# Chunk attention into a squared-ReLU FFN on one core: V loads moved from SyncE's queue to ACT's, from the second block on

## The chip, the cores and the metric

The kernel runs on one core of a Trainium2 chip. The metric is the device time of one execution in microseconds (us), as the median of several executions; the kernel before and the kernel under test run in turn on the same chip. The medians are over all runs of a kernel, a few of which were slow (2 of 4 in e7, 3 of 20 in e9b and in e15); the ratios are over fast runs alone. Engines are TensorE (PE; PEld is its weight load), VectorE (DVE), ScalarE (ACT), GpSimd (POOL) and SyncE (SP); "SPq" and "ACTq" in a profile are DMA issues of those two.

## The reference

Attention within chunks of 64 tokens, 8 heads of 64, over 8 x 576 tokens, then a two-layer FFN on the 4608 x 512 result. Cut to what matters:

```python
scores = scale * np.matmul(q_c, k_c.transpose(0, 1, 2, 4, 3))   # chunks of 64 x 64
attn = softmax(scores)                                          # (written out in the original)
out = np.matmul(attn, v_c)
x = out.transpose(0, 2, 1, 3).reshape(4608, 512)
h = np.maximum(x @ w_in, 0.0)                                   # 512 -> 2048
return (h * h @ w_out)                                          # 2048 -> 512
```

All inputs and the output are float32; the kernel computes in bf16.

## The kernel before

Tokens go in groups of 256 and blocks of two groups, 0 to 8. While PE works on the FFN of block j, the attention of block j+1 (`nxt`) is woven into it, and q, k and V of block j+2 (`far`) are loaded, cast and transposed. Each phase is a generator, and one step of it is a slot: `ffn_in` gives 16 slots, `ffn_out` another 16 (slots 16 to 31).

```python
NV = 5                                  # V buffers: 5 groups of even heads
NO = 2 * NV + 1                         # and 11 half-shifted tiles of odd heads
in_pool = tc.tile_pool(name="qk", bufs=5)
ps_ffn = tc.tile_pool(name="ps_ffn", bufs=4, space=PSUM)    # four banks
...
def v_pieces(g):                        # 4 or 5 DMAs a group, rows of 64 floats
    for t, p, m, b, s in runs(g):
        yield lambda ...: nc.sync.dma_start(out=v_even[g % NV][...], in_=v[...])
    for n in ...:
        ...
            yield lambda ...: nc.sync.dma_start(out=v_odd[n % NO][...], in_=v[...])
...
def transpose_qk_dma(g):                # "TD" in the plan: qkb (bf16) -> qkT
    ...
    nc.sync.dma_start_transpose(out=qkT..., in_=qkb...)
...
def transpose_x(g):                     # "XT": two of these a group, from group 6 on
    ...
            nc.sync.dma_start_transpose(out=xTs[j]..., in_=x...)
...
def ffn_in(j, c, n):                    # per slot: 4 matmuls, relu on ACT, square on DVE
    ...
def ffn_out(j):                         # per 4 slots: 16 matmuls into one bank, then
    ...
                o_sb = ffn_pool.tile([128, d_model], FP32, name="o_sb", bufs=4)
                nc.scalar.copy(out=o_sb, in_=o_ps)
                nc.scalar.dma_start(out=out[t0:t0 + 128, :], in_=o_sb)
```

The loop over blocks, for block 2 on:

```python
loads, go_slots = pieces(far), range(32)            # q, k of both groups, then V of both
d = {2: 5, 3: 2}.get(j, 0)
...                     # of nxt, from slot 4 + d: scores (SC), attention times V (AV), XT
for i, g in enumerate(far):
    at(14 + 2 * i, C, g)                            # cast of q and k on GpSimd
    at(19 + 3 * i, TD, g)                           # transpose of q and k by DMA
phases = [ffn_in(j, 0, len(grps) * GT), ffn_out(j)]
```

Every semaphore is set by the compiler. One thing about them: it gives all DMAs that SyncE and ACT issue one of eight completion semaphores, in turn, for both queues together. A DMA may reuse its semaphore only when the DMA eight places earlier has landed, so it waits for that one at its issuer. I call that one its eight-back partner. The traces bear this out: the DMA issues of the two engines carry eight semaphores in turn.

The softmax here doesn't subtract the row's maximum and nothing guards it: scores larger than these inputs give would overflow.

Of the kernel before, what the change touches and what calls it, by code (L numbers as in the profile page):

```python
# [17 lines left out]
def kernel(  # L18
# [9 lines left out]
    nc = tc.nc  # L28
# [46 lines left out]
    def segments(g0, n):  # L75
        while n:
            b, s = divmod(g0, S)
            m = min(n, S - s)
            yield b, s, m
            g0 += m  # L80
            n -= m
# [3 lines left out]
    def runs(g):  # L85

        for t in range(GT // 128):
            p = 0
            for b, s, m in segments(g * GT + t * 128, 128):
                yield t, p, m, b, s  # L90
                p += m

    def qk_pieces(g):
        q_sb = in_pool.tile([128, 2, H, D], FP32, name="q_sb")
        k_sb = in_pool.tile([128, 2, H, D], FP32, name="k_sb")
        qk[g] = (q_sb, k_sb)
        if g < FIRST_DMA_T:

            p = 0
            for b, s, m in segments(g * GT, GT):  # L100
                for dst, src in ((q_sb, q), (k_sb, k)):
                    yield lambda dst=dst, src=src, b=b, s=s, p=p, m=m: nc.sync.dma_start(
                        out=dst.rearrange("p t h d -> p (t h d)")[p:p + m // 2, :].rearrange(
                            "p (h e) -> p h e", h=H),
                        in_=src[b, :, s:s + m, :].rearrange("h (s i) d -> s h (i d)", i=2))
                p += m // 2
            return
        for t, p, m, b, s in runs(g):
            for dst, src in ((q_sb, q), (k_sb, k)):
                yield lambda dst=dst, src=src, b=b, s=s, t=t, p=p, m=m: nc.sync.dma_start(  # L110
                    out=dst[p:p + m, t, :, :],
                    in_=src[b, :, s:s + m, :].rearrange("h s d -> s h d"))

    def v_pieces(g):

        for t, p, m, b, s in runs(g):
            yield lambda t=t, p=p, m=m, b=b, s=s: nc.sync.dma_start(  # L117
                out=v_even[g % NV][p:p + m, t, :, 0:D],
                in_=v[b, 0::2, s:s + m, :].rearrange("h s d -> s h d"))
        for n in {0: [0, 1, 2], 2: [5], 3: [6, 7, 8]}.get(g, [2 * g + 1, 2 * g + 2]):  # L120
            lo, hi = max(0, 128 * n - 64), min(n_tokens, 128 * n + 64)
            p = lo - (128 * n - 64)
            for b, s, m in segments(lo, hi - lo):
                yield lambda n=n, p=p, m=m, b=b, s=s: nc.sync.dma_start(  # L124
                    out=v_odd[n % NO][p:p + m, :, 0:D],
                    in_=v[b, 1::2, s:s + m, :].rearrange("h s d -> s h d"))
                p += m

    def go(pieces):
        for f in pieces:  # L130
            f()
# [180 lines left out]
    def ffn_in(j, c, n):  # L312
        if j not in gTs:
            gTs[j] = ffn_pool.tile([128, n_ft, BT], BF16, name="gT")
        gT, xT = gTs[j], xTs[j]
        for ft in range(n_ft):
            h = ps_ffn.tile([128, 512], FP32, name="ps_ffn")
            for dt in range(n_dt):
                nc.tensor.matmul(  # L319
                    out=h[:, 0:n],  # L320
                    lhsT=w_in_bf[:, dt, ft * 128:(ft + 1) * 128],
                    rhs=xT[:, dt, c:c + n],
                    start=(dt == 0), stop=(dt == n_dt - 1))
            rl = ffn_pool.tile([128, 512], BF16, name="rl", bufs=3)
            nc.scalar.activation(out=rl[:, 0:n], in_=h[:, 0:n], func=AF.Relu)  # L325
            nc.vector.tensor_tensor(  # L326
                out=gT[:, ft, c:c + n], in0=rl[:, 0:n], in1=rl[:, 0:n], op=ALU.mult)
            yield

    def ffn_out(j):  # L330
        gT = gTs.pop(j)
        for tt in range(len(blocks[j]) * GT // 128):
            o_ps = ps_ffn.tile([128, d_model], FP32, name="ps_ffn")
            for ft in range(n_ft):
                nc.tensor.matmul(  # L335
                    out=o_ps,
                    lhsT=gT[:, ft, tt * 128:(tt + 1) * 128],
                    rhs=w_out_bf[:, ft, :],
                    start=(ft == 0), stop=(ft == n_ft - 1))
                if ft == n_ft - 1:  # L340
                    t0 = blocks[j][tt // 2] * GT + tt % 2 * 128
                    if j == len(blocks) - 1 and tt == 2 * len(blocks[j]) - 1:
                        for copy, dma, c in ((nc.scalar.copy, nc.scalar, 0),
                                             (nc.vector.tensor_copy, nc.sync, 256)):
                            o_sb = ffn_pool.tile([128, d_model], FP32, name="o_sb", bufs=4)
                            copy(out=o_sb[:, 0:256], in_=o_ps[:, c:c + 256])
                            dma.dma_start(
                                out=out[t0:t0 + 128, c:c + 256], in_=o_sb[:, 0:256])
                        yield
                        continue  # L350
# [3 lines that stand above are left out]
                if ft % 4 == 3:  # L354
                    yield
# [27 lines left out]
    def pieces(grps):  # L383
        for g in grps:
            yield from qk_pieces(g)
        for g in grps:
            yield from v_pieces(g)
# [27 lines left out]
    for j, grps in enumerate(blocks):  # L415
        nxt = blocks[j + 1] if j + 1 < len(blocks) else []
        far = blocks[j + 2] if j + 2 < len(blocks) else []
        plan = {}

        def at(slot, f, g):  # L420
            plan.setdefault(slot, []).append((f, g))

        if j == 0:
            loads, go_slots = iter(()), []
            for slot, f in ((24, T), (27, SC), (29, AV), (31, XT)):
                at(slot, f, nxt[0])
            at(31, T, nxt[1])
            phases = [ffn_in(0, 0, 512), ffn_out_by_ft(0)]
        elif j == 1:
            go_slots = [*range(17), *range(34, 48)]  # L430
            loads = itertools.chain(pieces(nxt), pieces(far))
            for slot, f in ((2, SC), (6, AV), (11, XT)):
                at(slot, f, grps[1])
            for i, g in enumerate(nxt):
                for slot, f in ((22 + 4 * i, C), (27 + 4 * i, TD), (36, SC), (38 + 2 * i, AV),
                                (42 + 2 * i, XT)):
                    at(slot, f, g)
            phases = [ffn_in(1, 0, 256), ffn_in(1, 256, 256), ffn_out(1)]
        else:
            loads, go_slots = pieces(far), range(32)  # L440
            d = {2: 5, 3: 2}.get(j, 0)
            if j == 2:
                go_slots = [*range(10), *range(18, 32)]
            for i, g in enumerate(nxt):
                for slot, f in ((4, SC), (8, AV), (11, XT)):
                    at(slot + d if f is SC else slot + d + 3 * i, f, g)
            for i, g in enumerate(far):
                at(14 + 2 * i, C, g)
                at(19 + 3 * i, TD, g)
            phases = [ffn_in(j, 0, len(grps) * GT), ffn_out(j)]  # L450
        slot = 0
        for phase in phases:
            for _ in phase:
                if slot in go_slots:
                    for f in loads:
                        f()
                        break
                for f, g in plan.get(slot, []):
                    f(g)
                slot += 1  # L460
        go(loads)
        if j == 1:
            for g in far:
                C(g)
                TD(g)
# [30 lines left out]
```

## Time and profile before

303.29 us was the median of the three runs before the change (300.78 to 303.96). The profiled run took 304.47 us.

| | before |
|---|---|
| span of the profiled run | 302.7 us |
| PE busy | 280.5 us, 93% |
| ACT busy | 130.0 us, 43% |
| PE starts ffn_in of blocks 2 to 8 at (timeline) | 89.58, 120.65, 151.15, 181.30, 212.52, 241.88, 271.24 |
| DMA queue q1 (SyncE), q10 (ACT) | 46.81 MB, 9.83 MB |

A block without a hole takes PE 29.36 us. Idle time of ACT or SyncE costs nothing by itself: what counts is what PE waits for. The lines are in the prediction.

### The profile page before, as it was taken

The numbers are of one execution on the slowest core, as the hardware profiler recorded it, in microseconds if no ns is written. First come the engines' busy times: TensorE is split into PE (matmuls) and PEld (weight loads), VectorE is DVE, ScalarE is ACT, GpSimd is POOL, SyncE is SP. The second block draws the span as 40 slices with busy tenths as digits, with TensorE's granted clock in tenths as the row PEclk, the third lists the DMA queues.
The fourth block names the chain that finished last, engine by engine and source line by source line (L and its number), as shares of the span: only waits on it lengthen the run. The fifth ranks groups of instructions, "written<-read, shape, count | busy, mean of one in ns | idle before, by whom it ended". The sixth has DMA issues, their size and how long they took to land.

```text
span 302.7 us, 6379 instructions
## 1 busy us (share of the span) xinstructions
PE 280.5 (93%) x2564; PEld 141.3 (47%) x2598; DVE 113.0 (37%) x247; ACT 130.0 (43%) x225; POOL 49.4 (16%) x68
## 2 busy tenths in 40 slices
PE   2889979898899799899999997999999999999995
PEld 2654435784454444444444443444444444444442
DVE  1348613692234350353037203740482038104400
ACT  1536305674217621762176215731662186217511
POOL 2047820140130040023003201400230000000000
PEclk9999999999799999999999999999999999999999
DMA  7999999999999899999899899869997704211011
GB/s 207 243 347 365 342 264 246 237 206 212 217 213 211 194 191 205 224 215 193 195 250 211 148 229 269 171 104 254 267 183 157 182 37 37 69 69 38 0 69 69
DMA packets 158765, 57.04 MB, mean 188 GB/s; under 512 B 139664, under 2 KB 152208, under 8 KB 158736
## 3 DMA queue, kind: packets, MB, share of 16 engines
q1 hardware_dynamic: 153024, 46.81, 73.2%
q10 hardware_dynamic: 5712, 9.83, 10.4%
q8 instruction: 20, 0.33, 0.5%
q14 instruction: 9, 0.07, 0.1%
HBM read 36.70 MB, written 9.44 MB: 152 GB/s over the span
## 4 chain that ended last, share of the span: by engine, by line
PE 67%; DMA 18%; SPq 10%; issue 2%; POOL 1%; ACT 1%; DVE 0%; ACTq 0%
PE ps_ffn L319 31%; PE ps_ffn L335 27%; DMA qkT<-qkb 6%; DMA k_sb<-in_k_dram 6%; SPq L224 4%; DMA w_st<-in_moe_w_in_dram 4%; SPq L282 3%; PE ps_att L259 2%; PE ps_ffn L364 2%; DMA w_st<-in_moe_w_out_dram 2%; PE ps_att L238 2%; SPq L117 1%; PE ps_ffn L164 1%; SPq L124 1%; POOL w_in_bf L139 1%
## 5 line engine op out<-in xcount | busy, mean ns | idle before, releaser
L319 PE MATMUL ps_ffn<-xT,w_in_bf 128*128 128x512 bf16 (+1 forms) x620 | 128.6, 357 | 3.1 <-ACT rl L325 1.6
L326 DVE TENSOR_TENSOR gT<-rl 128x512 bf16<-128x512 bf16 (+1 forms) x160 | 75.5, 489 | 133.9 <-ACT rl L325 131.4
L335 PE MATMUL ps_ffn<-w_out_bf,gT 128*128 128x512 bf16 x500 | 113.0, 382 | 0.8 <-issue 0.3
L325 ACT ACTIVATE rl<-ps_ffn 128x512 bf16<-128x512 f32 (+1 forms) x160 | 86.2, 560 | 42.5 <-PE ps_ffn L319 31.0
L319 PEld LDWEIGHTS <-w_in_bf 128*128 128x128 bf16 x640 | 60.8, 98 | 60.9 <-issue 2.1
L335 PEld LDWEIGHTS <-gT 128*128 128x128 bf16 x512 | 49.9, 98 | 59.7 <-issue 1.3
L352 ACT COPY o_sb<-ps_ffn 128x512 f32<-128x512 f32 x31 | 18.2, 586 | 92.9 <-PE ps_ffn L335 79.7
L217 POOL CAST qkb<-q_sb 128x1024 bf16<-128x1024 f32 x14 | 14.7, 1048 | 146.9 <-DMA q_sb<-in_q_dram 126.6
L269 DVE TENSOR_TENSOR x<-ps_att,rec 128x512 bf16<-128x512 f32 x36 | 24.9, 691 | 1.2
L245 ACT ACTIVATE e<-ps_att 128x1024 bf16<-128x1024 f32 x18 | 18.2, 1037 | 5.5 <-PE ps_att L238 5.5
L217 POOL CAST qkb<-k_sb 128x1024 bf16<-128x1024 f32 x14 | 16.0, 1144 | 6.5 <-DMA k_sb<-in_k_dram 6.4
L364 PE MATMUL ps_ffn<-w_out_bf,gT 128*128 128x512 bf16 x62 | 14.4, 379 | 0.2 <-issue 0.2
L238 PE MATMUL ps_att<-qkT 64*64 64x64 bf16 x576 | 8.1, 198 | 6.0 <-DMA qkT<-qkb 4.6
L266 DVE RECIPROCAL rec<-ps_att 128x8 f32<-128x8 f32 x36 | 7.1, 199 | 15.4 <-PE ps_att L259 15.4
L139 POOL CAST w_in_bf<-w_st 128x1024 bf16<-128x1024 f32 (+1 forms) x9 | 8.8, 980 | 19.1 <-DMA w_st<-in_moe_w_in_dram 19.1
L238 PEld LDWEIGHTS <-qkT 64*64 64x64 bf16 x576 | 6.2, 110 | 10.8 <-DMA qkT<-qkb 6.1
L259 PEld LDWEIGHTS <-e 64*64 64x64 bf16 x576 | 6.8, 110 | 8.5 <-DVE x L269 3.0
L259 PE MATMUL ps_att<-vo_sb,e 64*64 64x65 bf16 x288 | 9.2, 199 | 0.8 <-DMA vo_sb<-in_v_dram 0.8
L364 PEld LDWEIGHTS <-gT 128*128 128x128 bf16 x64 | 6.0, 98 | 7.2 <-issue 0.3
L147 POOL CAST w_out_bf<-w_st 128x1024 bf16<-128x1024 f32 x8 | 8.7, 1091 | 2.7 <-DMA w_st<-in_moe_w_out_dram 2.6
L259 PE MATMUL ps_att<-ve_sb,e 64*64 64x65 bf16 x288 | 9.2, 199 | 0.0
L173 ACT COPY qkT<-ps_att 128x512 bf16<-128x512 bf16 x4 | 2.1, 589 | 13.9 <-DVE qkT L173 11.8
(31 smaller groups left out, 46.0 us busy)
## 6 DMA issues: line engine op xcount, KB each, us to landing
out_dram<-o_sb ACTq DMA_DIRECT2D x35, 256.0 KB, 3.3
q_sb<-in_q_dram SPq DMA_DIRECT2D x25, 256.0 KB, 4.8
k_sb<-in_k_dram SPq DMA_DIRECT2D x25, 256.0 KB, 5.3
ve_sb<-in_v_dram SPq DMA_DIRECT2D x32, 128.0 KB, 3.9
vo_sb<-in_v_dram SPq DMA_DIRECT2D x32, 128.0 KB, 3.9
w_st<-in_moe_w_out_dram SPq DMA_DIRECT2D x8, 512.0 KB, 5.7
w_st<-in_moe_w_in_dram SPq DMA_DIRECT2D x7, 512.0 KB, 7.3
q_sb<-in_q_dram SPq DMA_DIRECT2D x3, 512.0 KB, 6.6
```

Source lines behind the costliest of these rows:

```text
L217: nc.gpsimd.tensor_copy(out=qkb[:, which], in_=qk[g][which].rearrange("p t h d -> p (t h d)"))
L224: nc.sync.dma_start_transpose(out=qkT.rearrange("c w t h q -> c (w t h) q"), in_=qkb.rearrange("p w c -> p (w c)"))
L238: nc.tensor.matmul(out=ps[64 * c:64 * c + 64, o0:o0 + 64], lhsT=qkT[64 * a:64 * a + 64, 1, t, hp, cols], rhs=qkT[64 * a:64 * a + 64, 0, t, ...
L245: nc.scalar.activation(out=e.rearrange("p a h t q -> p (a h t q)"), in_=ps, func=AF.Exp, scale=scale)
L259: nc.tensor.matmul(out=ps[64 * p:64 * p + 64, a, hp * (D + 1):(hp + 1) * (D + 1)], lhsT=e[64 * c:64 * c + 64, a, hp, t, :], rhs=vb[64 * c: ...
L269: nc.vector.tensor_tensor(out=x.rearrange("p h a d -> p a h d"), in0=o[:, :, :, 0:D], in1=rec.to_broadcast([128, 2, n_hp, D]), op=ALU.mult)
L319: nc.tensor.matmul(out=h[:, 0:n], lhsT=w_in_bf[:, dt, ft * 128:(ft + 1) * 128], rhs=xT[:, dt, c:c + n], start=(dt == 0), stop=(dt == n_dt ...
L325: nc.scalar.activation(out=rl[:, 0:n], in_=h[:, 0:n], func=AF.Relu)
L326: nc.vector.tensor_tensor(out=gT[:, ft, c:c + n], in0=rl[:, 0:n], in1=rl[:, 0:n], op=ALU.mult)
L335: nc.tensor.matmul(out=o_ps, lhsT=gT[:, ft, tt * 128:(tt + 1) * 128], rhs=w_out_bf[:, ft, :], start=(ft == 0), stop=(ft == n_ft - 1))
L352: nc.scalar.copy(out=o_sb, in_=o_ps)
L364: nc.tensor.matmul(out=o_ps[tt], lhsT=gT[:, ft, tt * 128:(tt + 1) * 128], rhs=w_out_bf[:, ft, :], start=(ft == 0), stop=(ft == n_ft - 1))
```

## The change

Its intent: SyncE issues all loads and transposes one after the other and runs late. V, which nothing needs soon, goes to the queue of ACT, in ffn_out, where ACT has little to do. The core of the diff:

```diff
-    def v_pieces(g):
+    def v_pieces(g, eng=nc.sync):
...
-            yield lambda t=t, p=p, m=m, b=b, s=s: nc.sync.dma_start(
+            yield lambda t=t, p=p, m=m, b=b, s=s: eng.dma_start(
...
         elif j == 1:
-            go_slots = [*range(17), *range(34, 48)]
-            loads = itertools.chain(pieces(nxt), pieces(far))
+            go_slots, v_slots = [*range(17), *range(34, 48)], range(34, 48)
+            loads = itertools.chain(pieces(nxt), *map(qk_pieces, far))
...
         else:
-            loads, go_slots = pieces(far), range(32)
-            d = {2: 5, 3: 2}.get(j, 0)
-            if j == 2:
-                go_slots = [*range(10), *range(18, 32)]
+            go_slots, v_slots = range(16), range(17, 32)
+            loads = itertools.chain(*map(qk_pieces, far))
+            d = {2: 5, 3: 2}.get(j, 1)
...
+        v_loads = itertools.chain(*(v_pieces(g, nc.scalar) for g in far if j))
...
-                if slot in go_slots:
-                    for f in loads:
-                        f()
-                        break
+                for queue, slots in ((loads, go_slots), (v_loads, v_slots)):
+                    if slot in slots:
+                        for f in queue:
+                            f()
+                            break
```

More of the change, by code (lines that the diff above doesn't have):

```diff
@@ L123, in v_pieces @@
             for b, s, m in segments(lo, hi - lo):
-                yield lambda n=n, p=p, m=m, b=b, s=s: nc.sync.dma_start(
+                yield lambda n=n, p=p, m=m, b=b, s=s: eng.dma_start(
                     out=v_odd[n % NO][p:p + m, :, 0:D],
@@ L423 @@
         if j == 0:
-            loads, go_slots = iter(()), []
+            loads, go_slots, v_slots = iter(()), [], []
             for slot, f in ((24, T), (27, SC), (29, AV), (31, XT)):
@@ L461 @@
         go(loads)
+        go(v_loads)
         if j == 1:
```

## The prediction

> **What bounds the kernel now.** I read the page's busy table first, then the table of stretches, then the waits of the tensor engine (PE), and from each wait the timeline of the queue that caused it.
>
> ```profile
> PE 280.5 (93%) x2564; PEld 141.3 (47%) x2598; DVE 113.0 (37%) x247; ACT 130.0 (43%) x225; POOL 49.4 (16%) x68
> ```
>
> PE is busy 280.5 of 302.7 us, so no change outside PE can gain more than 22 us, and most of that is the cold start (the first 20 us hold 7.5 us of it). The stretches show where the rest lies:
>
> ```profile
> 70.00:80.00 10.00, 8.12 (x114) 3.59 (x118) 0.45 (x2) 2.90 (x4) 0.00 (x0) 0.86 1.19 216
> 90.00:100.00 10.00, 8.77 (x70) 3.93 (x69) 4.25 (x10) 7.29 (x12) 0.00 (x0) 1.00 0.87 200
> 120.00:130.00 10.00, 8.95 (x101) 4.31 (x102) 2.98 (x7) 7.00 (x11) 0.00 (x0) 1.00 1.17 213
> 150.00:160.00 10.00, 9.34 (x104) 4.41 (x103) 2.98 (x7) 6.78 (x11) 0.00 (x0) 1.00 1.06 232
> 180.00:190.00 10.00, 8.37 (x99) 3.89 (x99) 2.76 (x5) 4.63 (x8) 1.98 (x2) 1.00 1.17 273
> 250.00:260.00 10.00, 9.89 (x105) 4.60 (x106) 6.95 (x18) 5.10 (x9) 0.00 (x0) 1.00 0.45 54
> ```
>
> The first number after the length is PE busy, then PE loads, DVE, ACT and POOL; the last three are granted clock, DMA share and GB/s. One hole per block of 512 tokens, and none once the loads are over. The first ffn_in matmuls of blocks 2 to 8 in PE's timeline give the same as lengths: they start at 89.74, 120.65, 151.15, 181.30, 212.68, 242.04 and 271.40, so blocks 2 to 7 last 30.91, 30.50, 30.15, 31.38, 29.36 and 29.36 us. The last two have no hole. Blocks 2 to 5 lose 1.55 + 1.14 + 0.79 + 2.02 = 5.5 us against 29.36. That is all this change can win there; block 1 (the hole at 70:80) lies before its first moved load.
>
> Three of the four holes (blocks 2, 3, 4) are PE waiting for qkT from the DMA transpose. SyncE's own timeline ahead of block 4's wait:
>
> ```profile
> 138.84 1.05 SPq L124 DMA_DIRECT2D vo_sb<-in_v_dram  x2
> 140.00 2.54 SPq L282 DMA_TRANSPOSE xT<-x  x2
> 142.59 1.93 SPq L117 DMA_DIRECT2D ve_sb<-in_v_dram  x3
> 144.62 2.55 SPq L282 DMA_TRANSPOSE xT<-x  x2
> 147.22 1.12 SPq L124 DMA_DIRECT2D vo_sb<-in_v_dram  x2
> 148.45 6.15 SPq L224 DMA_TRANSPOSE qkT<-qkb  x2
> ```
>
> Columns: start, length, what was issued, how many. There is no gap: the queue only issues. The cast that the second qkT transpose needs ended at 141.3 on POOL, yet the first is issued at 148.45. Its data lands at 156.56, and
>
> ```profile
> 156.60 0.45 PE L238 MATMUL ps_att<-qkT 64*64 64x64 bf16 x32 [0.60 <-DMA qkT<-qkb]
> ```
>
> So SyncE is late by its backlog, not by its inputs. Block 5's hole is another thing, on ACT:
>
> ```profile
> 178.18 0.59 ACT L352 COPY o_sb<-ps_ffn 128x512 f32<-128x512 f32 x1 [2.92 <-PE ps_ffn L335]
> 182.94 0.34 ACTq L353 DMA_DIRECT2D out_dram<-o_sb  x1
> 183.37 0.59 ACT L352 COPY o_sb<-ps_ffn 128x512 f32<-128x512 f32 x1 [4.61 <-PE ps_ffn L319]
> 185.52 0.34 ACTq L353 DMA_DIRECT2D out_dram<-o_sb  x1
> 185.96 2.56 ACT L325 ACTIVATE rl<-ps_ffn 128x512 bf16<-128x512 f32 x5 [2.00 <-DMA k_sb<-in_k_dram]
> ```
>
> ACT's copy is done at 178.77, but its store is issued at 182.94, the next at 185.52, and only then come the relus that PE waits for (1.57 us). The waits name a k load, which this store doesn't use. The compiled program explains it: the DMAs of both queues share eight completion semaphores in program order, so each waits at its issuer for the DMA eight before it. A late SyncE thus holds up ACT.
>
> **What the Trainium skill says.** All four points are from "DMA: Bandwidth & Descriptors". "Issuing engines are not separate DMA queues": a second issuing engine saves only the sequencer's time. The trace can't show two loading queues yet, but it gives that time: 606 and 595 ns median for a V issue, against 3.9 us to landing. "Anatomy of one DMA": a semaphore wait is served by the issuing sequencer before dispatch. The trace agrees: ACT stood 4.17 us between copy and store. "Queues, rings and completion order": each DMA engine takes turns between rows with work, packet by packet; no part of this trace has two heavy rows. "Why small descriptors are slow (HBM only)": 256-byte rows carry 27% overhead. V's rows are 64 floats, 256 bytes; the trace agrees in direction (139664 of 158765 packets are under 512 B; 207 GB/s at share 0.97 in 60:70, against 360 at 1.09 in 20:30 where 1 KB weight rows flow). The change alters neither bytes nor row size.
>
> **The change, part by part.**
>
> *Removed from SyncE.* V of the blocks loaded in blocks 1 to 6: groups 6 to 17, which the loop's segments cut into 9, 9, 9, 9, 9 and 8 issues, 53 of 80. In SyncE's timeline the nine V issues of blocks 2 to 5 took 5.5, 7.0, 6.1 and 6.7 us, mean 6.3. Per block SyncE now has about 9 q/k issues (0.95 us each by their line's medians: 8.6), four xT transposes (1.21: 4.8), two qkT (2.55: 5.1) and V (6.3), in all 24.8 of 29.4 us before any wait; with waits it was full. Without V: 18.5 us. The backlog of blocks 2 to 4 should go, and qkT of block 4, say, be issued about 5 us earlier, against a PE wait of 0.6.
>
> *Moved.* In ffn_out ACT has four copies (0.59) and four stores (0.34), 3.7 us of 13.8. Nine V issues add 9 x 0.70 = 6.3: 10 of 13.8. They start at slot 17, one a slot (0.86 us), and end by slot 26; the next relu is due at slot 32. The buffers are free (each V ring holds five groups, its last reader ran a block ago). The added waits are the eight-back ones. Counting DMAs by hand through slots 0 to 31: the fourth to sixth V wait for the four xT transposes (issued from slot 12 to 18, landing 3.1 us later, so by about slot 22); the ninth waits for the first qkT transpose (issued about slot 20, landing 4.9 us later, slot 26). ACT stands a few slots, with copies held up at most about 2 us, and a PSUM bank is asked for again only four banks later (3.45 us per bank in ffn_out). In block 2, whose attention is five slots later, the ninth V waits until about slot 28 to 30: closer, but before slot 32.
>
> *Changed.* The delay d of blocks 4 on goes from 0 to 1 slot (0.86 us later for scores and the rest): nothing for PE, whose work is the same, and some slack for qkT.
>
> *Block 1.* V runs beside the ffn_out of block 1, where DMA share is already 1.2 to 1.3 and q/k for the same groups are issued in the same slots. The bytes are the same, q/k just share with V, and by the eight-back rule q/k and V wait for each other. Casts ended at 89.4 before; they may end about 93 now. So of block 2's 1.55 us I count 0.4.
>
> *Sum.* Block 2: 0.4; block 3: 1.1; block 4: 0.8; block 5: 2.0 (the store's wait should go with SyncE's backlog). Together 4.3. I take off 0.8 for new waits on ACT at the ends of blocks 1 and 2. Gain 3.5 us: 303.29 - 3.5 = 299.8.
>
> **Rivals.** (1) *ACT becomes the wait.* V's issue can take up to 4.07 us (the maximum of that line) when DMA is pressed, and ACT serves relu, exp and copies in order; in block 1 the exponentials of two groups lie among the V issues. The ACT timeline above shows that 4 us of standing cost PE 1.6. If each of blocks 1 to 6 lost 1.5 us so, the gain would turn into +5: 304 to 308. Against it: V is issued only where ACT was 18% busy (1.76 us in 170:180). (2) *DMA is the bound*, and qkT is late whoever issues V. For it: share 0.9 to 1.2 in blocks 1 to 4. Then nothing moves: 302 to 304. Against it: in 190:240 share is 0.76 to 1.15, with the same bytes per block and no PE hole. (3) *More than I count:* the granted clock dips to 0.86 in 70:80, worth about 1.7 us (by 2 us stretches: 0.79, 0.50, 0.85 at 76 to 82). Its stretch precedes the change, but if it shifts away too, and block 2 gets its whole 1.55, I reach about 297.
>
> **Range and chances.** Three runs of before spread from 300.78 to 303.96, 1%, so I allow about 1 us of noise on top of 0 to 5.5 us of gain and a tail for rival 1: 296.9 to 303.4. Faster by over 2% means below 297.2, which needs every hole closed and a little more: 8%. Slower by over 2% means above 309.4, which needs rival 1 at its worst: 4%. Within: 88%.
>
> **What would show it.** Queue q1 should fall from 46.81 MB to 40.5 (12 groups x 0.524 MB moved), q10 rise from 9.83 to 16.1 MB. SyncE's timeline should have gaps from block 3 on, with qkT issued in the middle of ffn_out. Waits of PE on qkT: block 1's 1.7 us stays, the later three nearly vanish; block 5's wait on rl vanishes. Blocks 3 to 7 should each last 29.4 us. I am wrong if SyncE is still packed (rival 2), or if PE waits for rl, e or a bank while ACT stands before a V issue (rival 1).

## The result, and the profile after

The changed kernel takes 314.8 us (median of 4 runs, 313.23 to 317.35) against 302.12 for the kernel before. The ratio is 1.042 (95% interval 1.032 to 1.053): slower. Ratios here are the mean time of one kernel's fast runs over that of the other's in the same rounds, so not quite the ratio of the medians.

The busy row of the page and the stretches, with the columns as in the prediction:

```profile
PE 284.5 (90%) x2564; PEld 143.4 (45%) x2598; DVE 112.1 (36%) x247; ACT 128.4 (41%) x225; POOL 49.5 (16%) x68
```

```profile
90.00:100.00 10.00, 7.66 (x65) 3.47 (x64) 5.10 (x10) 6.67 (x11) 2.36 (x2) 1.00 1.10 179
...
120.00:130.00 10.00, 6.75 (x30) 2.83 (x29) 0.00 (x0) 1.48 (x3) 1.04 (x1) 1.00 1.32 229
...
150.00:160.00 10.00, 8.39 (x39) 3.77 (x39) 0.00 (x0) 1.17 (x2) 0.74 (x1) 1.00 1.32 224
...
190.00:200.00 10.00, 6.78 (x91) 3.04 (x91) 2.56 (x6) 6.25 (x11) 2.73 (x3) 1.00 1.10 224
...
220.00:230.00 10.00, 6.55 (x30) 2.75 (x29) 1.05 (x3) 3.56 (x7) 2.08 (x2) 1.00 1.30 245
```

There is still one hole per block, and each is larger, at 1.6 to 3.5 us. PE starts ffn_in of blocks 2 to 8 at 88.50, 122.87, 156.29, 188.45, 221.46, 254.76 and 284.12. Blocks 2 to 6 thus last 34.37, 33.42, 32.16, 33.01 and 33.30 us, 166.3 in all; before it was 152.3. These five blocks hold the whole loss. Block 7, which loads nothing, takes 29.36 as before.

What moved is just what should have moved (queue, packets, MB, share of the 16 engines):

```profile
q1 hardware_dynamic: 127856, 40.58, 64.6%
q10 hardware_dynamic: 30880, 16.06, 22.2%
```

SyncE also got its time back. Its timeline in block 3 (start, length, what, how many):

```profile
139.65 5.76 SPq L282 DMA_TRANSPOSE xT<-x  x4
145.50 5.46 SPq L224 DMA_TRANSPOSE qkT<-qkb  x2
151.01 0.58 SPq L110 DMA_DIRECT2D q_sb<-in_q_dram  x1
151.65 0.59 SPq L110 DMA_DIRECT2D k_sb<-in_k_dram  x1
```

It had stood from 132.6 to 139.65, waiting for DVE's x. Then four transposes of x go out, two of q and k, and at once, five us ahead of its own block, the next block's q and k. Now ACT in the same stretch:

```profile
146.13 0.59 ACT L352 COPY o_sb<-ps_ffn 128x512 f32<-128x512 f32 x1 [2.86 <-PE ps_ffn L335]
146.75 0.36 ACTq L353 DMA_DIRECT2D out_dram<-o_sb  x1
147.15 1.57 ACTq L124 DMA_DIRECT2D vo_sb<-in_v_dram  x2
150.98 4.77 ACTq L117 DMA_DIRECT2D ve_sb<-in_v_dram  x2
155.79 0.59 ACT L352 COPY o_sb<-ps_ffn 128x512 f32<-128x512 f32 x1 [9.07 <-DMA ve_sb<-in_v_dram]
...
157.62 1.44 ACTq L124 DMA_DIRECT2D vo_sb<-in_v_dram  x2
159.10 0.59 ACT L352 COPY o_sb<-ps_ffn 128x512 f32<-128x512 f32 x1 [2.72 <-PE ps_ffn L319]
```

The row at 150.98 holds two V issues of 0.6 us, one at 150.98 and one at 155.15. The first starts when the first qkT transpose has landed (145.50 and 5.5 us), the second when the second has (147.23 and 7.9 us). The V issue at 157.62 uses nothing of k, yet the chain of waits puts it behind a k load of the next block (start, length, what; pieces under 0.1 us are left out of the chains here):

```profile
151.65 5.95 DMA k_sb<-in_k_dram
157.62 0.79 ACTq L124
158.45 0.61 ACTq L124
159.10 0.59 ACT o_sb L352
```

The copy of the third output bank is done at 159.7, and PE's timeline has the matmul that needs this bank right behind it:

```profile
159.74 2.55 PE L319 MATMUL ps_ffn<-xT,w_in_bf 128*128 128x512 bf16 x9 [1.55 <-ACT o_sb L352]
```

So the wait of PE on SyncE's transposes was exchanged for a longer one on ACT, and ACT's waits name DMAs of SyncE. The compiled programs show why. This is the order in which the two kernels hand out the eight semaphores for block 3, with the order that my hand count in the prediction comes to (X: x transpose, T: qkT transpose, V: V load, o: output store, q: a q or k load, of the next block where it stands right of the transposes):

```
before          V V V V X X V V V o X X V V T o T q o q q o q q   (all but o are SyncE's)
after           X X X X V T V T q o V q V V q V o q V V q V q o q o q
my hand count   X X X X V V o V T V V V T o V V V o o q q q ...
```

In the changed kernel the fifth and sixth V have the two qkT transposes eight places back, and the eighth V and the second and last store have q or k loads of the next block. In my count the ninth V had the first transpose, and nothing had a load of the next block.

The trace also gives how long ACT stood for each. In blocks 2 to 5 it stood 5.4, 3.5, 4.2 and 4.3 us in front of the V issue whose partner is the second qkT transpose. The waits for next-block loads behind it added nothing, 0.3, 1.2 and 1.1 us, because ACT came to most of them when those loads were nearly or already there. And the last store of blocks 2, 4 and 5 stood another 1.1 to 1.9 us, until a V load of its own block had landed, with the relus behind it. At the start of block 3 a bank and then a relu came late like this, with no next-block load in the chain:

```profile
127.07 2.12 PE L319 MATMUL ps_ffn<-xT,w_in_bf 128*128 128x512 bf16 x8 [2.31 <-ACT o_sb L352]
```

```profile
118.16 6.72 DMA qkT<-qkb
124.90 4.25 DMA ve_sb<-in_v_dram
129.23 0.36 ACTq L353
129.69 0.61 ACT rl L325
```

### The profile page after: what moved, and what is told of

Same layout as the page of the kernel before. It is cut to its first block, busy times and chain, and to the rows that moved or that the text cites.

```text
span 315.6 us, 6359 instructions
## 1 busy us (share of the span) xinstructions
PE 284.5 (90%) x2564; PEld 143.4 (45%) x2598; DVE 112.1 (36%) x247; ACT 128.4 (41%) x225; POOL 49.5 (16%) x68
## 3 DMA queue, kind: packets, MB, share of 16 engines
q1 hardware_dynamic: 127856, 40.58, 64.6%
q10 hardware_dynamic: 30880, 16.06, 22.2%
## 4 chain that ended last, share of the span: by engine, by line
PE 43%; DMA 24%; SPq 13%; DVE 9%; ACT 5%; issue 4%; ACTq 1%; POOL 0%
PE ps_ffn L319 24%; PE ps_ffn L335 10%; DMA k_sb<-in_k_dram 8%; SPq L224 8%; DMA ve_sb<-in_v_dram 6%; DMA vo_sb<-in_v_dram 5%; PE ps_ffn L364 4%; DMA qkT<-qkb 4%; DVE gT L326 4%; ACT rl L325 3%; DVE x L269 3%; SPq L282 2%; DMA q_sb<-in_q_dram 2%; PE ps_att L238 1%; SPq L102 1%
## 5 line engine op out<-in xcount | busy, mean ns | idle before, releaser
L319 PE MATMUL ps_ffn<-xT,w_in_bf 128*128 128x512 bf16 (+1 forms) x620 | 132.3, 360 | 13.6 <-ACT o_sb L352 6.8
L326 DVE TENSOR_TENSOR gT<-rl 128x512 bf16<-128x512 bf16 (+1 forms) x160 | 74.6, 483 | 148.9 <-ACT rl L325 145.5
L335 PE MATMUL ps_ffn<-w_out_bf,gT 128*128 128x512 bf16 x500 | 111.7, 379 | 0.8 <-issue 0.3
L325 ACT ACTIVATE rl<-ps_ffn 128x512 bf16<-128x512 f32 (+1 forms) x160 | 84.8, 559 | 43.3 <-PE ps_ffn L319 28.8
L217 POOL CAST qkb<-k_sb 128x1024 bf16<-128x1024 f32 x14 | 15.0, 1074 | 7.7 <-DMA k_sb<-in_k_dram 7.6
L364 PE MATMUL ps_ffn<-w_out_bf,gT 128*128 128x512 bf16 x62 | 14.4, 379 | 0.2 <-issue 0.2
```

The source lines that it names most:

```text
L217: nc.gpsimd.tensor_copy(out=qkb[:, which], in_=qk[g][which].rearrange("p t h d -> p (t h d)"))
L319: nc.tensor.matmul(out=h[:, 0:n], lhsT=w_in_bf[:, dt, ft * 128:(ft + 1) * 128], rhs=xT[:, dt, c:c + n], start=(dt == 0), stop=(dt == n_dt ...
L325: nc.scalar.activation(out=rl[:, 0:n], in_=h[:, 0:n], func=AF.Relu)
L326: nc.vector.tensor_tensor(out=gT[:, ft, c:c + n], in0=rl[:, 0:n], in1=rl[:, 0:n], op=ALU.mult)
L335: nc.tensor.matmul(out=o_ps, lhsT=gT[:, ft, tt * 128:(tt + 1) * 128], rhs=w_out_bf[:, ft, :], start=(ft == 0), stop=(ft == n_ft - 1))
L364: nc.tensor.matmul(out=o_ps[tt], lhsT=gT[:, ft, tt * 128:(tt + 1) * 128], rhs=w_out_bf[:, ft, :], start=(ft == 0), stop=(ft == n_ft - 1))
```

## The experiments

Twelve kernels ran, all with correct results, four at a time; each four has its own runs of the kernel before beside it.

| label | what it is | this, us | before, us | ratio (95%) |
|---|---|---|---|---|
| (the change) | V on ACT | 314.8 | 302.12 | 1.042 (1.032 to 1.053) |
| e1 | V on SyncE, new slots | 303.55 | 301.1 | 1.010 (1.007 to 1.013) |
| e2 | V on GpSimd | 313.92 | 301.1 | 1.044 (1.037 to 1.050) |
| e5 | V late on ACT | 338.84 | 301.1 | 1.127 (1.120 to 1.134) |
| e7 | half of V on ACT | 311.7 | 301.1 | 1.028 (1.016 to 1.040) |
| e9 | e1, block 1 as before | 299.13 | 300.88 | 0.996 (0.993 to 0.999) |
| e9b | e9, V behind the transposes | 299.43 | 300.88 | 0.995 (0.992 to 0.998) |
| e10 | e9 and nine copies on ACT | 298.89 | 300.88 | 0.994 (0.992 to 0.997) |
| e11 | e9b and two waits on ACT | 305.99 | 300.88 | 1.015 (1.009 to 1.021) |
| e12 | the change, q and k held to their block | 304.6 | 300.54 | 1.014 (1.008 to 1.019) |
| e13 | e11 with a longer scratch tile | 298.96 | 300.54 | 0.994 (0.990 to 0.997) |
| e14 | the change, block 1 as before | 309.89 | 300.54 | 1.031 (1.027 to 1.036) |
| e15 | e12 and e14 together | 301.12 | 300.54 | 1.002 (0.999 to 1.005) |

The fours ran on different chips, and the kernels before differ by up to 1.6 us, so a difference of medians across fours is rough. By the ratios, e1 is 9.9 us below the changed kernel, e12 8.6, e14 3.3 and e15 12.2, where the interval of the changed kernel's ratio alone spans 6 us.

The first theory was WAITS: ACT stands before a V issue because its eight-back partner, a DMA of SyncE, has not landed, and the output copies stand behind it. Its rivals were ISSUE TIME (nine V issues are too much for ACT) and CONTENTION (V beside the transposes slows them).

### e1, e2: V off ACT

```diff
-        v_loads = itertools.chain(*(v_pieces(g, nc.scalar) for g in far if j))
+        v_loads = itertools.chain(*(v_pieces(g) for g in far if j))             # e1
+        v_loads = itertools.chain(*(v_pieces(g, nc.gpsimd) for g in far if j))  # e2
```

> V goes back to SyncE, in the new slots (17 on). WAITS (ACT stands before a V issue because the DMA eight before it, often a transpose or a next-block q/k load of SyncE, has not landed, and the output copies stand behind it): 299 to 304 us, no wait of ACT's output copy on a V load. ISSUE TIME (nine V issues simply take too much of ACT): the same, 299 to 304. CONTENTION (V beside the transposes slows them on the DMA engines, because of when it is issued): 310 or more, as V still flows at the same time.

e1 took 303.55 us: 11.2 us less than the changed kernel by the medians, with nothing but the issuing engine changed. From 110 us on no 10 us stretch has less than 9.7 us of PE. CONTENTION by the time of issue falls. What is left is at the start of block 2: one wait for qkT of 4.4 us, and after it a clock of 0.70 in 100:110.

> V is issued by GpSimd in the same slots: still a second queue beside SyncE, but its completion semaphores are another set, and ACT has none of the issues. WAITS and ISSUE TIME: 297 to 303, ACT's copies wait only for PE. CONTENTION of two queues: 310 or more. Side risk: if a V issue takes GpSimd over 1.5 us, its casts come late and PE waits for qkT; then the waits name POOL.

e2 took 313.92 and so missed what I expected of it under both theories. Two things are in its trace. First, GpSimd issues block 1's nine V loads in one go, from 66.5 to 73.0, before and beside the two qkT transposes, whose issues then take 3.8 and 6.8 us (the median before is 2.55). PE waits for qkT, the clock falls to 0.53 and 0.50 in 78:82 and 82:86, and 70:90 holds 13.8 us of PE work in place of 18.0. That much looks like contention, at one place. Second, with V out of the count, ACT's own stores get q and k loads as eight-back partners (12 of 33, counted in the compiled order from block 1's weave on), those at the end of a block loads of the next. A store of ACT then stood from 182.47 to 187.11 for such a q load, until 2.0 us after block 5 had started, and a relu behind it waited too. That block lasted 31.7 us and the next, with the same wait, 32.8. In blocks 2 and 3 the third store stood for the second qkT transpose instead, but only until 1.5 and 0.8 us before the next block, and those next blocks lasted 29.4 us. So taking V off ACT is not enough; the stores are tied to SyncE too.

### e5, e7: when, and how much, on ACT

```diff
-            go_slots, v_slots = range(16), range(17, 32)
+            go_slots, v_slots = range(16), range(28, 32)                  # e5
```

e7 leaves `eng` out of the even-head loads only, so they go back to SyncE.

> V stays on ACT, but four pieces go in slots 28 to 31 and the rest after the block's last copy. The eight-back partner of a V issue is then a transpose in 4 of 48 cases instead of 18. WAITS: most of the loss goes, 300 to 306. ISSUE TIME: the same nine issues stand in front of the next relus in one lump, so 312 or more. CONTENTION: V flows after most of the transposes, so this also falls, to 305 or so; the landing times of the transposes tell it from WAITS.

e5 took 338.84: a clear miss for WAITS as I had put it, with transposes as the culprits. Only 4 of 53 V issues have a transpose eight back (18 in the changed kernel; the totals of 48 and 50 in the expectations are miscounts), and it is by far the slowest kernel. Its chain of waits around the start of block 4 shows the culprit:

```profile
160.70 7.12 DMA k_sb<-in_k_dram
167.84 0.61 ACTq L117
168.49 2.50 DMA ve_sb<-in_v_dram
170.99 0.60 ACT rl L325
171.64 3.55 PE ps_ffn L319 x8
```

A k load of the next block was in front of a V issue, and the V issues were in front of the relu. PE waited 28.4 us for relus in this run. As six of the nine V come after the last output copy here, nothing caught the wait: relu is what PE needs at once. ISSUE TIME had "312 or more" here and was not refuted by it.

> Only the odd-head V (4 or 5 of 9 issues a block) is on ACT, the even-head V back on SyncE. A transpose of qkT is the eight-back partner in 3 of about 25 V issues on ACT, instead of 9 of 48, and a next-block load in 2 instead of 17. WAITS: 301 to 305. ISSUE TIME: half the loss, 307 to 309. CONTENTION: most of the loss, 310 or more, as all of V still flows beside the transposes.

e7 took 311.7, but two of its four runs are slow; the fast ones are 307.31 and 311.38, above what WAITS expected and on both sides of the line between ISSUE TIME and CONTENTION. It doesn't tell the theories apart; its profiled run (305.5 us) has the same waits of PE on ACT's relu and copies (3.4 and 2.5 us), and a 3.6 us wait for qkT at the start of block 2 like e1.

### e9, e9b: a base without the loss

```diff
-            go_slots, v_slots = [*range(17), *range(34, 48)], range(34, 48)
-            loads = itertools.chain(pieces(nxt), *map(qk_pieces, far))
+            go_slots, v_slots = [*range(17), *range(34, 48)], []
+            loads = itertools.chain(pieces(nxt), pieces(far))
...
+        v_loads = itertools.chain(*(v_pieces(g) for g in far if j > 1))
...
+            go_slots, v_slots = range(16), range(23, 32)                  # e9b only
```

> The first run's kernel (V on SyncE, in the new slots) with block 1's loads in their old order, q, k and then V. The first run showed no PE hole from its block 3 on, but 4.4 us of PE waiting for qkT at the start of block 2 and a clock dip behind it. If that came from V taking SyncE's slots between q and k in block 1, this reads 297 to 300, faster than before by 1 to 2%. If it comes from elsewhere, 302 to 304.

e9 took 299.13, 4.4 us less than e1, and is faster than the kernel before by 0.4%, with an interval that leaves 1 out. So weaving V between q and k in block 1 costs about 4 us even on SyncE's own queue: the q and k loads, and with them the qkT transposes of block 2, come later.

> As the run before it, but V starts at slot 23, behind both qkT transposes in SyncE's order, which is when the transposes went out in the changed kernel. Base for the wait-only run. All theories: 297 to 301, with qkT issued right behind xT.

299.43, as expected: the transposes could be freed of SyncE's backlog without a second queue, by letting them go ahead of V.

### e10, e11, e13: ACT's time and ACT's waits, each alone

e10 is e9 with work for ACT and no DMA in it; e11 and e13 are e9b with waits and nearly no work.

```diff
+                if 2 <= j <= 6 and 17 <= slot < 26:                       # e10
+                    nc.scalar.copy(out=scr2, in_=scr)                     # 128 x 512 f32
...
+                if 2 <= j <= 6 and slot in (21, 22):                      # e11, e13
+                    g = far[slot == 22]
+                    nc.scalar.copy(out=scr[:, 0:8], in_=state["qkT", g][:, 0, 0, 0, 0:8])
```

> V on SyncE as in the first of this call, but ACT is given nine copies of 128x512 (0.5 to 0.6 us each) in slots 17 to 25 of blocks 2 to 6: the time of the nine V issues without their waits and without a second loading queue. WAITS: no change against its base, 297 to 301, since ACT has the room. ISSUE TIME: the loss comes back, 306 to 313.

298.89 against 299.13: nine copies a block, at a median of 0.62 us, cost nothing. ISSUE TIME falls, since a V issue on ACT took less (medians 0.59 and 0.52 us for even and odd heads in the changed kernel).

> V on SyncE behind the transposes, but in slots 21 and 22 of blocks 2 to 6 ACT reads 8 columns of the two qkT that are being transposed: two of the waits that ACT had in the changed kernel, without any V issue on ACT. WAITS: a good part of the loss comes back, 303 to 311 (the waits for the next block's q and k loads are not rebuilt), and ACT's output copies stand behind qkT. ISSUE TIME or CONTENTION: no change against its base, 297 to 301.

e11 took 305.99, as WAITS had it. But its trace did not: most of PE's loss is at the start of block 2, at 90 to 110 us, before the first added wait can act; the stretches from 110 to 250 lose only 1.2 us. The scratch tile was 16 bytes long and had shifted the buffers behind it, so I supposed, and I ran it again with 2 KB.

> The wait-only run again (ACT reads both qkT in slots 21 and 22, V on SyncE behind the transposes), with the scratch tile 2 KB long instead of 16 bytes: in the first one most of the PE loss lay at the start of block 2, before the first added wait, and only 1.2 us lay behind the waits. If that start was an accident of the buffers' addresses, this reads 299 to 302 (NEXT-BLOCK LOADS: waits in the middle of ffn_out are caught by the four PSUM banks). TRANSPOSES: 304 to 309 again, with the loss behind the waits.

298.96. In ffn_out ACT stands as it did in e11, but PE doesn't notice. ACT's timeline in block 3:

```profile
138.71 0.35 ACTq L354 DMA_DIRECT2D out_dram<-o_sb  x1
143.09 0.20 ACT L464 COPY scr<-qkT 128x8 bf16<-128x8 bf16 x1 [4.42 <-DMA qkT<-qkb]
145.16 0.20 ACT L464 COPY scr<-qkT 128x8 bf16<-128x8 bf16 x1 [1.87 <-DMA qkT<-qkb]
145.26 0.58 ACT L353 COPY o_sb<-ps_ffn 128x512 f32<-128x512 f32 x1
...
149.86 1.77 ACT L326 ACTIVATE rl<-ps_ffn 128x512 bf16<-128x512 f32 x3 [0.82 <-DMA ve_sb<-in_v_dram]
```

ACT waits 4.42 and 1.87 us for the two transposes (30.3 us in the ten waits of the run), does its copies late, and is there for the relus. So waits for the transposes are caught by the four PSUM banks when they end this early: here the second transpose lands 1.9 to 4.6 us before the next block starts, and no V is queued behind the wait. In the changed kernel it lands from 2.0 us after to 2.1 us before, and two or three further V issues and as many copies come behind the V that waits for it. So e13 doesn't clear the transposes there. I narrowed the theory to waits that come at the end of a block, and took these to be those for the next block's loads. (Why 16 bytes cost 7 us in e11 was not followed up.)

### e12, e14, e15: the narrowed theory

NEXT-BLOCK LOADS: ACT's last V issues and stores of a block wait for q and k loads that SyncE issues ahead of time, behind its transposes. The rival is TRANSPOSES. e12 keeps V on ACT, and keeps the transposes as partners (of other V issues, see below), but holds SyncE: ACT writes one column of the block's first q buffer at slot 0, so its load, and in SyncE's order all behind it, can't run ahead.

```diff
-            loads = itertools.chain(*map(qk_pieces, far))
+            loads = iter([f for g in far for f in qk_pieces(g)])
...
+                if j >= 2 and slot == 0 and far:
+                    nc.scalar.copy(out=qk[far[0]][0][:, 0, 0, 0:1], in_=ident_f32[:, 0:1])
```

e14 is the changed kernel with block 1 loaded as before (e9's edit, with V on ACT from block 2 on), and e15 has both edits. In the compiled order of e15, block 3 reads `X X V X X V T T o V V V V o V V V o o`, then the eight q and k of block 4: nothing of the next block in it. The two qkT transposes now belong to the seventh and eighth V, behind the second store, not to the fifth and sixth ahead of it; e12 has the same order.

> The changed kernel with one thing more: ACT writes one column of the first q buffer of a block at that block's slot 0, before its load, so SyncE can't run ahead into the next block's q and k loads. In the compiled order of completion semaphores the next block's loads then come behind all V loads and stores of the block; the transposes stay eight-back partners of V (24 of 50 V issues on ACT). NEXT-BLOCK LOADS (ACT stands at the end of a block because its last V issues and stores wait for q and k loads that SyncE could only issue after the transposes): from block 3 on the holes go, 300 to 306, what is left being block 2's start. TRANSPOSES (the waits for xT and qkT are what costs): 311 to 316, as changed.

304.6 us: holding SyncE back makes the changed kernel 10.2 us faster by the medians, though the transposes are still eight-back partners of 24 of 53 V issues. So the order of the semaphores is what costs. But the edit changes two things in that order, the next-block loads and the place of the transposes, so it doesn't show that the loads alone cost this much.

> The changed kernel with block 1 loaded as before (V of its second group pair on SyncE, behind q and k); V on ACT from block 2 on. This is block 1's part of the loss: the first run of the first call put it at 4 to 5 us against the same kernel with block 1 old. So 308 to 312 if parts add up; 313 to 316 if the holes of blocks 3 on only move.

309.89: block 1's part is 4.9 us by the medians and 3.3 by the ratios, around the 4 that e1 and e9 gave.

> Both repairs on the changed kernel: block 1 old, and q and k held to their own block; V still on ACT in slots 17 on, still behind transposes in the semaphore order. NEXT-BLOCK LOADS: 297 to 301, at or below the kernel before. TRANSPOSES: 306 to 312.

301.12, ratio 1.002: the loss is gone with V still on ACT. By the ratios the two repairs, 8.6 and 3.3, add up to the 12.2 that they gave together. The second transpose lands as late against the next block as in the changed kernel, from 2.3 us after its start to 1.7 us before, and a V issue (in block 2 a store) still stands for it; but behind it come at most one V and two copies. So a late transpose is not costly as such: it depends on what is queued behind it. ACT still waits in e15 (its copies 14.3 us for V issues, in three waits), and PE loses 0.25 us in each of the stretches around the start of block 4:

```profile
140.00:150.00 10.00, 9.73 (x46) 4.31 (x44) 0.00 (x0) 1.04 (x2) 0.00 (x0) 1.00 1.02 189
150.00:160.00 10.00, 9.75 (x134) 4.48 (x134) 4.75 (x12) 8.04 (x16) 0.82 (x1) 1.00 0.91 212
```

## Why the prediction was wrong

Predicted were 299.8 us in a range of 296.9 to 303.4; measured were 314.8. The range and the chance of 4% for "slower by over 2%" were both wrong. By its steps:

- **What bounds the kernel now: right.** SyncE's backlog held up the transposes. e9 and e9b, which move V later on the same queue (q and k to earlier slots, with the new kernel's `d`), take the holes of blocks 3 to 5 away (two for qkT, one on ACT). (The block starts given there mix two views, which differ by up to 0.16 us.) Even so the gain was 0.4 to 0.5%, 1.2 to 1.5 us of 301, not the 3.5 that I had as the sum; the 5.5 us of holes were those of a run of 304.47 us. ("Most of that is the cold start" is a wrong reading: 7.5 of 22 us is a third.)
- **Removed from SyncE: right.** q1 fell to 40.58 MB and q10 rose to 16.06 as worked out, and SyncE's timeline has gaps.
- **Moved, ACT's time: right in the mechanism.** I had 0.70 us an issue; it was 0.52 to 0.59, and e10 shows that this much work on ACT is free.
- **Moved, the eight-back waits: the step that failed.** "Counting DMAs by hand through slots 0 to 31" took the order of the slots for the order of the semaphores, and stopped at slot 31. The compiler's order is another: SyncE, freed of V, is ahead, so the next block's q and k loads come among the block's last V loads and stores. Their landing is late, as they are issued only after six transposes (11.2 us in block 3). I had the ninth V wait for the first qkT transpose; in truth the fifth and sixth wait for the two, with all the rest of the block's V queued behind, and later V issues and stores wait for loads of the next block. I had "copies held up at most about 2 us"; at 3.45 us a bank the second copy of block 3 was due at about 149.6 and came at 155.79, an estimated 6 us late. So PE waited 6.8 us for banks (before: none) and 4.9 us for relus (before: 1.6). Holding SyncE's loads to their own block, which changes both kinds of wait, gave back about 9 us (e12). How much each is worth in the changed kernel stays open: ACT stood longest for the transposes, while e2 and e5 show next-block waits at work where hardly a transpose is in front of ACT's late issues. A third effect isn't told apart either: e12 and e15 also keep next-block loads off the DMA engines while the last V of a block flows. That SyncE should be early was counted only as a gain; with shared semaphores its earliness is also what ties ACT to it.
- **"A PSUM bank is asked for again only four banks later": right, as far as e13 tests it.** It caught waits that ended over 1.9 us before the next block. It didn't catch the later ones of the changed kernel, and it can't help the relu (e5).
- **Block 1: wrong in sign.** I counted a gain of 0.4 us in block 2 "as q/k just share with V". The measured cost of the new block 1 is 3.3 to 4.9 us (e14), and e1 against e9 shows about 4 without ACT having a part in it. I had put the later end of the casts, "about 93", in the text and did not carry it on to block 2: in the changed kernel PE's longest wait for qkT is 3.1 us, at the start of block 2, where it was 1.4 before, and a clock dip follows (0.50 in 102:104).
- **Rivals.** Rival 1 was the one that came, with its sum (+5) less than half of what it cost; I set it aside because ACT is 18% busy there. Busy time was not the measure: an engine that stands at a semaphore is idle and blocked. Rival 2 is refuted for blocks 3 on by e9 and e15, which move the same bytes without these holes. Of rival 3, the clock dip of 70:80 did go (1.00 there), but another came in 100:110 (0.83).

## What to carry to other kernels

A second DMA queue is not independent of the first if both take their completion semaphores from one pool: look in the compiled order at which DMA each issue has to wait for, beyond the end of the iteration. Here reordering the loads on one queue, whose engine computes nothing (e9b), gave what little there was, and the second queue gave none of it. And a wait on an engine is judged by what stands behind it when it ends, not by its length: 6 us that ended in the middle of ffn_out were free (e13), while waits ahead of the next block's relus made the slowest kernel of all (e5).

## What the Trainium skill lacked or had wrong

- "DMA: Bandwidth & Descriptors", section "Issuing engines are not separate DMA queues", says that a second issuing engine saves only the sequencer's issue time. It doesn't say that it can cost more than it saves: the changed kernel lost 12.7 us by the medians, and about 9 of them came back by a single wait that reorders the shared completion semaphores (e12).
- "TensorE: Matmul & The Clock Gate", section "Part 1: The HAM clock gate", gives half clock after at least one idle window of about 3.4 us. By that row alone no dip would be expected here, yet shorter idleness did it in some cases: before, PE was busy 0.58 us in 74:76 with a longest wait of 1.67 us, and the clock was 0.50 in 78:80. A wait of 2.31 us at the start of block 3 in the changed kernel left the clock at 1.00. So the length of the longest wait doesn't tell whether a kernel pays for a dip. (A later section of the page tells of a dip from frequent short idling, but gives no length.)
- No page has this: a scratch tile of 16 bytes in place of 2 KB made a kernel take 306.0 us in place of 299.0, with the loss at the start of block 2 (e11, e13). The cause is open.
- No page says how a burst from GpSimd meets transposes in flight on another queue: nine V loads issued in 6.5 us, at a median of 0.75 us each, went with transpose issues of 3.8 and 6.8 us where 2.55 was the median before (e2).
